# RWKV attention and a top-1 MoE on one core: u terms per block, other load order, states of 48 columns, row loads in two parts

## The chip, the cores and the metric

The kernel runs on one core of one Trainium2 chip. The metric is the device time of one execution in microseconds (us). A core has five engines that run their own instruction streams: TensorE (PE), VectorE (DVE), ScalarE (ACT), GpSimd (POOL) and SyncE (SP), which here issues nearly all DMA transfers. In a trace every fp32 matmul stands as two records. The profiler also gives the TensorE clock that was granted, as a share of full speed; in this trace it stands at 1.0 (2.4 GHz) or at 0.5 (1.2 GHz).

## The reference

The inputs have batch B = 4, H = 8 heads, S = 768 steps and head size D = 48. The attention part is a recurrence over steps, and its output, seen as 3072 tokens of 384 values, goes into a mixture of experts with one expert for each token:

```python
for t in range(S):
    cur = np.einsum('bhd,bhe->bhde', u[None] * kt, vt)
    y[:, :, t] = np.einsum('bhd,bhde->bhe', rt, state + cur)
    state = wt[:, :, :, None] * state + np.einsum('bhd,bhe->bhde', kt, vt)
x = attn_out.transpose(0, 2, 1, 3).reshape(B * S, H * D)
logits = x @ w_gate                      # 3072 x 8
expert_idx = np.argmax(logits, axis=1)
gate_w = softmax(logits)[arange, expert_idx]
for e in range(E):                       # 8 experts, 384 -> 1024 -> 384
    mask = expert_idx == e
    out[mask] = gate_w[mask, None] * (np.maximum(x[mask] @ w1[e], 0.0) @ w2[e])
```

## The kernel before, in words

**Attention.** The 768 steps are cut into 6 chunks of 128, so there are 24 blocks; block n has chunk c = n // 4 and batch b = n % 4. The 8 heads of a batch lie as 4 pairs; a pair takes 112 partitions, one head in 0 to 47, the other in 64 to 111. For each block the host packs w, r and k of all heads into one row tile `rkwt` (112 x 1544) and the values into `vt` (128 x 384). Per block:

- DVE forms products of decays by a scan (`suf`, L294), their reciprocal, `kh` (L301) and a second scan `pre` (L303). POOL forms `rk` (L286), the product of r and k that the u term needs, and `rh` (L315).
- PE multiplies `rh` and `kh` (L384, tile `ap`: the decayed products of all pairs of steps). POOL fills two tiles `at` with the u terms on the diagonal and zeros elsewhere (L365, from `ct`), and DVE copies the strict triangle of `ap` over them (L386). The u terms come from `rk` by a matmul with `ubt` (L340, `cp`), a copy on ACT (L343, `cs`), a transpose (L352, `cpt`) and a second copy on ACT (L354, `ct`).
- PE adds up the output `yp`: first the part from the state of the chunks before (`inter`, L395: the state `gbd` of a pair is a block-diagonal 112 x 112 matrix whose off-diagonal blocks are zero, one matmul for a pair), then the part within the chunk (`av`, L424: `at` by `vt`). ACT copies it to `ytb` (L428; in the first chunk L432).
- PE forms the chunk's contribution to the state (`ds`, L406, tile `dp`), DVE adds it into `sst` (L413, or copies it in chunk 0, L415), and ACT multiplies by the chunk's decay into `gbd` for the next chunk (`prep_g`, L331, 4 instructions for a block).
- `y_tr` (L440) transposes `ytb` into rows of tokens, ACT copies those to `xr`; once per chunk the logits (L456), the routing and the place of each token follow, and POOL scatters the rows by indirect DMA into `xs` in DRAM, one area for each expert (`scatter`). Before that, `prefill` has filled the rows that no token may reach (8 DMAs from `zrow`, L279).

**Experts.** The weights come in 20 pieces for an expert through 3 staging buffers `wst` (L182, L185), and ACT and DVE split them into a high and a low part (L195, L196). `load_rows` (L211) loads the rows of an expert, `xg`, from `xs`; the partition dimension of the load is 112, 116, 108, 103, 99 or 97 by the expert's capacity (128 for the last, and 96 and 128 for the two parts of the first). PE transposes them (L246), multiplies by w1 (L255) and w2 (L778), and an indirect DMA writes the result (L217). The transpose at L246 is the first thing that an expert does on PE.

**Order.** A tile scheduler orders PE, DVE, ACT and POOL by the dependences and the program's order. SP issues in program order: a DMA whose buffer isn't free yet holds everything that stands behind it on SP. In the loop over the blocks, `load(n + 5)` and `load_v(n + 5)` follow block n; a tag has 6 buffers.

Of the kernel before, what the change touches and what calls it, by code (L numbers as in the profile page):

```python
# [43 lines left out]
def rwkv_moe_kernel(ctx, tc, rkw, vv, ub, wgp, wg, w1, w2, out):  # L44
# [62 lines left out]
    make_identity(nc, ident)  # L107
    pre0 = []
# [14 lines left out]
    for b in range(B):  # L123
        gbd[b] = acon.tile([RP, NP_, RP], F32, name=f"gbd{b}")
        t = acon.tile([RP, NP_, RP], F32, name=f"sst{b}")
        nc.gpsimd.memset(t, 0.0)
        sst.append(t)
# [82 lines left out]
    def load_rows(t, e, row, n, p):  # L210
        i = nc.sync.dma_start(t, xs[e, row:row + n, :].rearrange("e (p j) c -> p (e j) c", p=p))  # L211
        for k in scat:
            tc.add_manual_dep(i.ins, k.name, mybir.DependencyInfo(mybir.DependencyClass.Sync, mybir.DependencyReason.DATA),
                              reason="rows of all tokens")
# [118 lines left out]
    def coef_mm(c, bs=range(B)):  # L333
        if c >= NCH:
            return
        nb = len(bs)
        cp = psL.tile([32 * nb, C], F32, name="cp", tag="lg")
# [4 lines left out]
        cs = sm.tile([32 * nb, C], F32, name="cs", tag="cs")  # L342
        nc.scalar.activation(cs, cp, AF.Copy)  # L343
        for b in bs:
            ch["cs", c, b] = cs

    def coef_tr(c, bs=range(B)):
        if c >= NCH:
            return
        nb = len(bs)  # L350
        cp = psL.tile([P, 32 * nb], F32, name="cpt", tag="lg")
        nc.tensor.transpose(cp, ch["cs", c, bs[0]], ident[:32 * nb, :32 * nb])  # L352
        ct = sm.tile([P, nb, 32], F32, name="ct", tag="ct")
        nc.scalar.activation(ct.rearrange("p b h -> p (b h)"), cp, AF.Copy)  # L354
        for i, b in enumerate(bs):
            ch["ct", c, b] = ct[:, i, :]

    def diag(n):
# [4 lines left out]
        co = ch["ct", n // B, n % B]  # L363
# [24 lines left out]
    def inter(n):  # L388
# [215 lines left out]
    def coefs(c, bs):  # L604
        coef_mm(c, bs)
        coef_tr(c, bs)

    C0 = {0: (1,), 1: (2, 3)}
    coefs(0, (0,))
    diag(0)  # L610
    prep_r(1)
    prep_rk(2)
    prep_rk(3)
    for n in range(NB):
        c, b = divmod(n, B)
        kt(n)
        if b == 0 and c > 0:
            diag(n)
# [3 lines left out]
        if n in C0:  # L622
            with hp():
# [383 lines left out]
```

## Time and profile before

| | us |
|---|---|
| three runs, lowest, median, highest | 521.66, 525.41, 527.87 |
| the profiled execution | 524.86 |
| its span from the first to the last instruction | 523.1 |
| PE busy in it (share) | 449.3 (86%) |
| DVE busy (share) | 308.5 (59%) |
| ACT and POOL busy (share) | 189.6 (36%) and 190.2 (36%) |
| mean granted clock of TensorE | 0.878 |

The lines of 40 slices on the page show the course: attention takes slices 1 to about 18 (13.1 us each), with DVE nearly full in many of them and PE's clock moving between 0.5 and 1; then come the experts, where PE is nearly full and the clock falls in single slices. A window's row gives the busy time of each engine in it, the number of records, the mean granted clock and the share of the 16 DMA engines. A timeline row gives the start, the time and the instruction, and in square brackets how long the engine had been idle before it and what it waited for.

### The profile page before, as it was taken

To read this page: it belongs to the slowest core of one execution; us is meant where nothing else is said; L and a number is where in the kernel's file an instruction comes from. 1 tells how busy PE (TensorE), PEld (TensorE's weight loads), DVE (VectorE), ACT (ScalarE), POOL (GpSimd) and SP (SyncE) were. 2 spreads that over 40 slices of the span, in tenths; PEclk is the share of its full clock that TensorE was granted. 3 is DMA by queue.
4 is the path that set the end of the run, shared out by engine and by line. 5 is a ranking of instruction groups with operands and counts; after the bars stand their busy time and mean duration, and the time that the engine had idled before them with its cause. 6 is when DMAs were issued, how large, how long until landed. Compare 5 with 4: busy or idle time off the path is not lost.

```text
span 523.1 us, 8844 instructions
## 1 busy us (share of the span) xinstructions
PE 449.3 (86%) x3323; PEld 399.2 (76%) x3323; DVE 308.5 (59%) x555; ACT 189.6 (36%) x447; POOL 190.2 (36%) x203
## 2 busy tenths in 40 slices
PE   6689979488798969799689999993999939999992
PEld 6466768367676758588689998883999929999992
DVE  6998467489979899654567525331646306261320
ACT  4262423343352353223535525332445205242210
POOL 7766252187485876350521002100303005230341
PEclk9585557787898989799979999996999978999998
DMA  8934434657443961410556244232643242410020
GB/s 228 282 126 138 143 119 141 187 204 201 137 139 102 297 168 58 171 47 18 166 205 223 82 164 134 58 112 98 181 152 115 80 136 82 142 41 5 3 51 36
DMA packets 35174, 67.68 MB, mean 129 GB/s; under 512 B 7636, under 2 KB 22909, under 8 KB 35124
## 3 DMA queue, kind: packets, MB, share of 16 engines
q1 hardware_dynamic: 27220, 57.52, 35.8%
q0 software_dynamic: 7904, 9.52, 5.7%
q8 instruction: 28, 0.46, 0.4%
q14 instruction: 22, 0.18, 0.1%
HBM read 51.81 MB, written 15.63 MB: 129 GB/s over the span
## 4 chain that ended last, share of the span: by engine, by line
issue 35%; PE 29%; DVE 17%; DMA 8%; POOL 5%; SPq 3%; ACT 1%; POOLq 0%; DVEq 0%; ACTq 0%
PE bank L255 6%; PE ap L384 5%; DMA rkwt<-in_rkw_dram 5%; POOL out_dram L217 4%; DVE suf L294 4%; PE yp L424 3%; PE opt L267 3%; DMA out_dram<-ot,xg 2%; DVE kh L301 2%; PE bank L778 2%; PE yp L395 2%; DVE pre L303 2%; DVE at L386 2%; PE yq L440 2%; PE lp L456 1%
## 5 line engine op out<-in xcount | busy, mean ns | idle before, releaser
L217 POOL DMA_INDIRECT out_dram<-ot,xg x24 | 37.2, 1551 | 177.0 <-DVE ot L768 171.5
L196 DVE TENSOR_TENSOR w2l<-wst,w2h 128x512 fp32r<-128x512 f32 x48 | 34.1, 745 | 64.4 <-ACT w2h L195 64.2
L384 PE MATMUL ap<-rh,kh 48*128 48x128 f32 (+1 forms) x384 | 61.8, 327 | 9.3 <-DVE pre L299 5.2
L384 PEld LDWEIGHTS ap<-rh,kh 48*128 48x128 f32 (+1 forms) x384 | 51.9, 224 | 19.1 <-DVE at L386 8.2
L255 PE MATMUL bank<-xl,w1h 128*128 128x448 f32 (+6 forms) x168 | 60.0, 361 | 0.0
L255 PE MATMUL bank<-xh,w1l 128*128 128x448 f32 (+6 forms) x168 | 58.6, 354 | 0.0
L255 PE MATMUL bank<-xh,w1h 128*128 128x448 f32 (+6 forms) x168 | 57.8, 368 | 0.3 <-ACT xh L247 0.3
L286 POOL TENSOR_TENSOR rk<-rkwt 112x512 f32<-112x512 f32 x24 | 37.0, 1542 | 31.3 <-DMA rkwt<-in_rkw_dram 20.2
L258 DVE SCALAR_TENSOR_TENSOR hl<-bank,hh 128x192 fp32r<-128x192 f32 (+8 forms) x58 | 30.5, 539 | 28.3 <-ACT hh L257 28.3
L424 PE MATMUL yp<-at,vt 128*48 128x128 f32 x384 | 40.7, 322 | 6.1 <-DVE at L386 6.1
L257 ACT ACTIVATE hh<-bank 128x192 fp32r<-128x192 f32 (+8 forms) x58 | 26.8, 477 | 42.7 <-PE bank L255 41.9
L365 POOL TENSOR_SCALAR_AFFINE_SELECT at<-ct 128x512 f32<-128x512 f32 x48 | 40.3, 866 | 5.0 <-PE yp L424 4.8
L294 DVE TENSOR_TENSOR_SCAN suf<-rkwt,sufone 112x520 f32<-112x520 f32 x24 | 38.8, 1619 | 5.4 <-DMA rkwt<-in_rkw_dram 5.2
L778 PE MATMUL bank<-hl,w2h 128*128 128x412 f32 (+5 forms) x114 | 40.8, 359 | 0.0
L778 PE MATMUL bank<-hh,w2l 128*128 128x412 f32 (+5 forms) x114 | 40.6, 358 | 0.0
L386 DVE COPY_PREDICATED at<-cmask,ap 128x512 f32<-128x512 int32 x48 | 34.2, 720 | 9.9 <-PE ap L384 9.1
L778 PE MATMUL bank<-hh,w2h 128*128 128x412 f32 (+5 forms) x114 | 39.8, 355 | 0.0
L196 DVE TENSOR_TENSOR w1l<-wst,w1h 128x512 fp32r<-128x512 f32 x48 | 31.0, 686 | 14.2 <-ACT w1h L195 14.1
L424 PEld LDWEIGHTS yp<-at,vt 128*48 128x48 f32 x384 | 28.0, 145 | 14.4 <-DVE at L386 8.8
L195 ACT ACTIVATE w2h<-wst 128x512 fp32r<-128x512 f32 x48 | 27.5, 623 | 31.6 <-DMA wst<-in_w_dram 28.9
L303 DVE TENSOR_TENSOR_SCAN pre<-rkwt,pre 112x520 f32<-112x520 f32 x24 | 35.1, 1461 | 4.7 <-POOL rh L315 4.1
L315 POOL TENSOR_TENSOR rh<-rkwt,pre 112x512 f32<-112x512 f32 x22 | 28.4, 1292 | 25.8 <-PE yp L395 16.9
(153 smaller groups left out, 928.2 us busy)
## 6 DMA issues: line engine op xcount, KB each, us to landing
rkwt<-in_rkw_dram SPq DMA_DIRECT2D x23, 675.5 KB, 18.7
wst<-in_w_dram SPq DMA_DIRECT2D x48, 256.0 KB, 5.6
wst<-in_w_dram SPq DMA_DIRECT2D x16, 768.0 KB, 7.5
xs<-zrow SPq DMA_DIRECT2D x7, 699.6 KB
vt<-in_vv_dram SPq DMA_DIRECT2D x24, 192.0 KB, 6.5
xg<-xs SPq DMA_DIRECT2D x1, 699.6 KB
xs<-zrow SPq DMA_DIRECT2D x1, 675.5 KB
xg<-xs SPq DMA_DIRECT2D x1, 675.5 KB
```

The source lines that it names most:

```text
L196: nc.vector.tensor_tensor(out=lo, in0=st[:, cs], in1=hi.bitcast(F32), op=ALU.subtract)
L217: i = nc.gpsimd.indirect_dma_start(out=out[:, :], out_offset=bass.IndirectOffsetOnAxis(ap=t.bitcast(I32)[:, q, DM + 1:DM + 2], axis=0), in ...
L255: nc.tensor.matmul(hp, a, x[:, j, :], start=(i == 0), stop=(i == 8))
L258: nc.vector.scalar_tensor_tensor(out=hl, in0=hp, scalar=0.0, in1=hh.bitcast(F32), op0=ALU.max, op1=ALU.subtract)
L286: return nc.gpsimd.tensor_tensor(out=d["rk"], in0=d["r"], in1=d["k"], op=ALU.mult)
L294: nc.vector.tensor_tensor_scan(out=suf[:, ::-1], data0=w[:, ::-1], data1=sufone.rearrange("p q c -> p (q c)")[:, ::-1], initial=0.0, op0=A ...
L303: nc.vector.tensor_tensor_scan(out=pre, data0=w, data1=p0.rearrange("p q c -> p (q c)"), initial=0.0, op0=ALU.mult, op1=ALU.add)
L365: nc.gpsimd.affine_select(out=at[:, j], in_=co[:, j:H:2].unsqueeze(2).broadcast_to([P, NP_, C]), pattern=[[0, NP_], [-1, C]], compare_op=A ...
L384: nc.tensor.matmul(ap[j][:, q, :], d["kh"][rs, q, :], d["rh"][rs, q, :], start=True, stop=True)
L386: nc.vector.copy_predicated(out=d["at"][:, j], mask=cmask.unsqueeze(1).broadcast_to([P, NP_, C]), data=ap[j])
L424: nc.tensor.matmul(yp[64 * j:64 * j + D, q, :], d["v"][:, h * D:(h + 1) * D], d["at"][:, j, q, :], start=(c == 0 and q == 0), stop=(q == N ...
L778: nc.tensor.matmul(pp, w, a, start=(i == 0), stop=(i == 23))
```

## The change

Four things are changed. (1) A row load whose partition count isn't a multiple of 16 becomes two: up to the last multiple of 16, and the rest. (2) `load` runs 6 blocks ahead instead of 5, `load_v` 3 instead of 5, `prefill` goes from blocks 0 to 7 to blocks 2 to 9, the first two scatters go to blocks 11 and 12. (3) The u terms are formed for each block, one block ahead: four matmuls put the four pairs into four column groups of one 128-row tile, ACT copies it whole, a matmul with the constant 128 x 8 matrix `pick` adds up what belongs to a head and transposes in one step, ACT copies the 128 x 8 result; `rk` is formed 2 blocks ahead instead of 4. (4) `gbd` and `sst` hold 48 columns for a head (and 64 in memory) in place of 112 with a zero half; `inter` becomes 8 matmuls of 64 or 48 rows instead of 4 of 112; `ds` fills 64 rows for the first head of a pair, and `sst` takes one DVE instruction over 112 partitions for a block in place of two over 48.

```diff
+    pick = const.tile([P, H], F32, name="pick")
+    nc.vector.tensor_reduce(out=pick, in_=ident.rearrange("p (q h) -> p h q", q=NP_)[:, 0:H, :], axis=AX.X, op=ALU.add)
...
-        gbd[b] = acon.tile([RP, NP_, RP], F32, name=f"gbd{b}")
-        t = acon.tile([RP, NP_, RP], F32, name=f"sst{b}")
-        nc.gpsimd.memset(t, 0.0)
-        sst.append(t)
+        gbd[b] = acon.tile([RP, NP_, 64], F32, name=f"gbd{b}")
+        sst.append(acon.tile([RP, NP_, D], F32, name=f"sst{b}"))
...
     def load_rows(t, e, row, n, p):
-        i = nc.sync.dma_start(t, xs[e, row:row + n, :].rearrange("e (p j) c -> p (e j) c", p=p))
+        src = xs[e, row:row + n, :].rearrange("e (p j) c -> p (e j) c", p=p)
+        m = p - p % 16
+        for ps in ((slice(0, m), slice(m, p)) if m < p else (slice(0, p),)):
+            i = nc.sync.dma_start(t[ps], src[ps])
...
-            nc.scalar.activation(d["g"][:, q, :], sst[n % B][:, q, :], AF.Copy, scale=d["wt"][:, q:q + 1])
+            nc.scalar.activation(d["g"][:, q, 0:D], sst[n % B][:, q, :], AF.Copy, scale=d["wt"][:, q:q + 1])
...
+    def coef_mm(n):
+        cp = psL.tile([P, C], F32, name="cp", tag="lg")
         for q in range(NP_):
-            for i, b in enumerate(bs):
-                nc.tensor.matmul(cp[32 * i:32 * i + 32, :], ubt[:, q, :], blk[c * B + b]["rk"][:, q, :],
-                                 start=(q == 0), stop=(q == NP_ - 1))
+            nc.tensor.matmul(cp[32 * q:32 * q + 32, :], ubt[:, q, :], blk[n]["rk"][:, q, :], start=True, stop=True)
+        cs = sm.tile([P, C], F32, name="cs", tag="cs")
         nc.scalar.activation(cs, cp, AF.Copy)
+        blk[n]["cs"] = cs
+
+    def coef_tr(n):
+        cp = psL.tile([P, H], F32, name="cpt", tag="lg")
+        nc.tensor.matmul(cp, blk[n]["cs"], pick, start=True, stop=True)
+        ct = sm.tile([P, H], F32, name="ct", tag="ct")
+        nc.scalar.activation(ct, cp, AF.Copy)
+        blk[n]["ct"] = ct
...
-                nc.tensor.matmul(yp[:, q, :], d["g"][:, q, :], d["rh"][:, q, :],
-                                 start=(q == 0), stop=False, skip_group_check=True)
+                for j in range(2):
+                    m = 64 if j == 0 else D
+                    rs = slice(64 * j, 64 * j + m)
+                    nc.tensor.matmul(yp[rs, q, :], d["g"][rs, q, 0:m], d["rh"][rs, q, :],
+                                     start=(q == 0), stop=False, skip_group_check=True)
...
-                    nc.tensor.matmul(dp[64 * j:64 * j + D, q, :], d["kt"][:, q * RP + 64 * j:q * RP + 64 * j + D],
+                    m = 64 if j == 0 else D
+                    nc.tensor.matmul(dp[64 * j:64 * j + m, q, :], d["kt"][:, q * RP + 64 * j:q * RP + 64 * j + m],
...
-            for j in range(2):
...
-                    nc.vector.tensor_tensor(out=s[rs, :, cs], in0=dp[rs], in1=d["g"][rs, :, cs], op=ALU.add)
...
+                nc.vector.tensor_tensor(out=s, in0=dp, in1=d["g"][:, :, 0:D], op=ALU.add)
...
+        with hp():
+            coefs(n + 1)
+        prep_rk(n + 2)
+        diag(n + 1)
...
-            if c > 1:
+            if c > 2:
                 scatter(c - 1)
...
-        load(n + 5)
-        load_v(n + 5)
-        if n == E:
-            scatter(0)
+        load(n + 6)
+        load_v(n + 3)
+        if n in (11, 12):
+            scatter(n - 11)
...
-        if n < E:
-            prefill(n)
+        if 2 <= n < 2 + E:
+            prefill(n - 2)
```

On SP, in the first blocks (rkwt are the packed inputs of a block, vt its values, xs the prefilled rows), the order before is this:

```order
L75 DMA rkwt<-in_rkw_dram 112x1544
L84 DMA vt<-in_vv_dram 128x384
L279 DMA xs<-zrow 448x1x386
L75 DMA rkwt<-in_rkw_dram 112x1544
L84 DMA vt<-in_vv_dram 128x384
L279 DMA xs<-zrow 464x1x386
```

and now:

```order
L75 DMA rkwt<-in_rkw_dram 112x1544 x4
L84 DMA vt<-in_vv_dram 128x384
L75 DMA rkwt<-in_rkw_dram 112x1544
...
L282 DMA xs<-zrow 448x1x386
L75 DMA rkwt<-in_rkw_dram 112x1544
L84 DMA vt<-in_vv_dram 128x384
```

Four packed inputs now go out in a row, the values stand three blocks behind them, and the prefill starts two blocks later.

On PE, one block of the second chunk (yq is the transpose of the block before, yp the block's output, dp the state's new part, kp a transpose of kh, ap the products of the next block) before:

```order
L340 MATMUL cp<-rk,ubt 32x128 x2
L440 MATMUL yq<-ident,ytb_203 128x112 x4
L395 MATMUL yp<-rh,gbd_189 112x128 x4
L406 MATMUL dp<-vt,kt 48x48 x8
L374 MATMUL kp<-ident,kh 128x112 x4
L424 MATMUL yp<-at,vt 48x128
L384 MATMUL ap<-rh,kh 128x128 x4
L424 MATMUL yp<-at,vt 48x128 x7
```

and the same place now:

```order
L340 MATMUL cp<-rk,ubt 32x128 x4
L368 MATMUL kp<-ident,kh 128x112 x4
L378 MATMUL ap<-rh,kh 128x128 x4
L435 MATMUL yq<-ident,ytb_201 128x112 x4
L392 MATMUL yp<-rh,gbd_189 64x128
L392 MATMUL yp<-rh,gbd_189 48x128
...
L347 MATMUL cpt<-pick,cs 128x8
L404 MATMUL dp<-vt,kt 64x48
L404 MATMUL dp<-vt,kt 48x48
```

The product with the state alternates between the two halves of the array (three more pairs of such rows are left out), the state's new part does the same, and the u terms' matmuls and their transpose by pick now stand in every block.

On SP in the experts (ISA rows are register work of the load), before:

```order
L702 TENSOR_LOAD order
L702 REGISTER_ALU x3
L702 ISA
L211 ISA
L211 DMA xg<-xs 103x1544
L185 ISA
L185 DMA wst<-in_w_dram 128x4x384
```

and now:

```order
L688 TENSOR_LOAD order
L688 REGISTER_ALU x3
L688 ISA
L214 ISA
L214 DMA xg<-xs 96x1544
L214 ISA
L214 DMA xg<-xs 7x1544
L185 ISA
L185 DMA wst<-in_w_dram 128x4x384
```

The one load of 103 partitions has become one of 96 and one of 7, at the same place ahead of the weights.

## Rows read from the trace of the kernel before

**Rows 1.** The head of the page: span, busy time of each engine, and the line of the granted clock over 40 slices.

```profile
span 523.1 us, 8844 instructions
...
PE 449.3 (86%) x3323; PEld 399.2 (76%) x3323; DVE 308.5 (59%) x555; ACT 189.6 (36%) x447; POOL 190.2 (36%) x203
...
PEclk9585557787898989799979999996999978999998
```

**Rows 2.** Busy time by stretch of the attention part: window, its length, busy us and records of PE, PEld, DVE, ACT and POOL, granted clock, DMA share, GB/s. Block 0 ends about the end of the first row; the rows then hold blocks 1 to 3, 4 to 7, 8 to 19 and 20 to 23.

```profile
0.00:30.30 30.30, 21.46 (x190) 17.39 (x191) 25.81 (x39) 10.03 (x25) 21.94 (x46) 0.72 0.82 226
30.30:55.20 24.90, 22.47 (x162) 16.70 (x162) 21.45 (x28) 11.37 (x31) 14.50 (x14) 0.70 0.46 143
55.20:106.40 51.20, 40.95 (x347) 32.73 (x348) 30.54 (x53) 19.38 (x53) 18.29 (x22) 0.68 0.51 157
106.40:210.50 104.10, 89.59 (x966) 73.87 (x966) 95.74 (x165) 43.38 (x123) 71.90 (x75) 0.89 0.53 161
210.50:238.00 27.50, 24.26 (x216) 19.39 (x216) 15.14 (x38) 5.78 (x17) 10.61 (x14) 0.88 0.30 104
```

**Rows 3.** Timeline of ACT: the copies of yp to ytb that end blocks 7 and 19.

```profile
106.35 0.60 ACT L428 ACTIVATE ytb<-yp 112x512 f32<-112x512 f32 x1 [0.72 <-PE yp L424]
...
210.49 0.58 ACT L428 ACTIVATE ytb<-yp 112x512 f32<-112x512 f32 x1
```

**Rows 4.** Timeline of PE in the experts: the first transposes of the rows of two experts.

```profile
361.12 0.58 PE L246 MATMUL pt<-ident,xg 103*128 103x103 f32 x2 [9.11 <-DMA xg<-xs]
...
431.79 0.56 PE L246 MATMUL pt<-ident,xg 97*128 97x97 f32 x2 [9.27 <-DMA xg<-xs]
```

**Rows 5.** Timeline of SP: when the loads of those rows were issued.

```profile
332.17 0.29 SPq L211 DMA_DIRECT2D xg<-xs  x1
...
404.53 0.29 SPq L211 DMA_DIRECT2D xg<-xs  x1
```

**Rows 6.** Windows in the experts, columns as in rows 2: one while the first of the two loads runs, and the stretches right behind the two waits.

```profile
336.00:338.00 2.00, 2.00 (x11) 1.80 (x10) 0.00 (x0) 0.00 (x0) 0.00 (x0) 1.00 0.07 28
...
361.00:364.30 3.30, 3.18 (x12) 3.07 (x13) 0.61 (x2) 1.27 (x3) 0.00 (x0) 0.50 0.07 27
...
431.80:436.00 4.20, 4.20 (x16) 4.20 (x17) 1.63 (x3) 2.29 (x5) 0.00 (x0) 0.50 0.08 28
```

**Rows 7.** SP's own waits over the whole span: waited for, total us, times, longest.

```profile
SPq L84 <- PE yp L424: 82.9, 12, 11.8
...
SPq L84 <- PE dp L406: 27.4, 4, 10.5
```

**Rows 8.** Timelines of SP, ACT, PE and POOL about the end of the second chunk.

```profile
86.90 6.62 SPq L182 DMA_DIRECT2D wst<-in_w_dram  x3
...
99.96 0.63 ACT L195 ACTIVATE w1h<-wst 128x512 fp32r<-128x512 f32 x1 [7.38 <-DMA wst<-in_w_dram]
...
101.13 1.01 PE L440 MATMUL yq<-ident,ytb 112*128 112x112 f32 x4 [6.96 <-ACT ytb L428]
...
103.40 1.85 POOL L286 TENSOR_TENSOR rk<-rkwt 112x512 f32<-112x512 f32 x1 [10.05 <-DMA rkwt<-in_rkw_dram]
```

**Rows 9.** Groups of instructions by line and form over the whole span: count, busy us, mean ns of one, idle time before them and what ended it.

```profile
L331 ACT ACTIVATE gbd<-sst,wtot 112x112 f32<-112x112 f32 x80 | 25.4, 378 | 28.8 <-DVE sst L413 28.1 <-PE yp L395 0.5
...
L413 DVE TENSOR_TENSOR sst<-dp,gbd 48x192 f32<-48x192 f32 x32 | 11.2, 349 | 1.9 <-PE dp L406 1.7
...
L415 DVE COPY sst<-dp 48x192 f32<-48x192 f32 x8 | 2.7, 343 | 0.1
...
L459 ACT ACTIVATE ls<-lp 128x128 f32<-128x128 f32 x6 | 1.6, 272 | 3.7 <-PE lp L456 3.7
...
L352 PE MATMUL cpt<-ident,cs 128*128 128x128 f32 x5 | 1.6, 329 | 0.0
```

**Rows 10.** Timeline of PE in the second chunk: the products with the state (L395), within the chunk (L384, L424), each line so many records in a row. The first two stand in stretches at clock 0.5, the other three in one at 1.0.

```profile
61.97 2.05 PE L395 MATMUL yp<-rh,gbd 112*112 112x128 f32 x8
...
82.89 1.80 PE L395 MATMUL yp<-rh,gbd 112*112 112x128 f32 x8
...
85.63 1.71 PE L384 MATMUL ap<-rh,kh 48*128 48x128 f32 x16
...
88.58 1.04 PE L395 MATMUL yp<-rh,gbd 112*112 112x128 f32 x8
89.55 1.08 PE L424 MATMUL yp<-at,vt 128*48 128x128 f32 x16
```

**Rows 11.** Windows between changes of the clock, from block 2 to block 6, columns as in rows 2.

```profile
40.20:61.90 21.70, 20.72 (x145) 15.05 (x144) 15.14 (x22) 7.38 (x20) 8.80 (x8) 0.50 0.48 152
61.90:64.00 2.10, 2.10 (x11) 2.03 (x11) 0.00 (x0) 1.40 (x4) 0.00 (x0) 0.51 0.27 97
64.00:67.30 3.30, 1.81 (x30) 1.22 (x28) 2.86 (x9) 2.05 (x7) 3.13 (x5) 1.00 0.47 121
67.40:82.80 15.40, 13.99 (x88) 10.99 (x89) 9.85 (x22) 2.38 (x5) 5.05 (x6) 0.50 0.37 121
...
84.50:94.20 9.70, 9.38 (x114) 7.59 (x112) 7.04 (x8) 3.90 (x11) 4.96 (x6) 1.00 0.47 143
```

**Rows 12.** Timeline of DVE in the first blocks: the two masked copies that finish the first block's at.

```profile
22.55 0.74 DVE L386 COPY_PREDICATED at<-cmask,ap 128x512 f32<-128x512 int32 x1
...
25.59 0.73 DVE L386 COPY_PREDICATED at<-cmask,ap 128x512 f32<-128x512 int32 x1
```

More of the change, by code (lines that the diff above doesn't have):

```diff
@@ L210, in load_rows @@
     def load_rows(t, e, row, n, p):
-        i = nc.sync.dma_start(t, xs[e, row:row + n, :].rearrange("e (p j) c -> p (e j) c", p=p))
-        for k in scat:
-            tc.add_manual_dep(i.ins, k.name, mybir.DependencyInfo(mybir.DependencyClass.Sync, mybir.DependencyReason.DATA),
-                              reason="rows of all tokens")
+        src = xs[e, row:row + n, :].rearrange("e (p j) c -> p (e j) c", p=p)
+        m = p - p % 16
+        for ps in ((slice(0, m), slice(m, p)) if m < p else (slice(0, p),)):
+            i = nc.sync.dma_start(t[ps], src[ps])
+            for k in scat:
+                tc.add_manual_dep(i.ins, k.name, mybir.DependencyInfo(mybir.DependencyClass.Sync, mybir.DependencyReason.DATA),
+                                  reason="rows of all tokens")
     def scatter_out(t, q, rows):
@@ L330, in prep_g @@
         for q in range(NP_):
-            nc.scalar.activation(d["g"][:, q, :], sst[n % B][:, q, :], AF.Copy, scale=d["wt"][:, q:q + 1])
[L333 to L337, printed above, removed]
+            nc.scalar.activation(d["g"][:, q, 0:D], sst[n % B][:, q, :], AF.Copy, scale=d["wt"][:, q:q + 1])
+    def coef_mm(n):
+        cp = psL.tile([P, C], F32, name="cp", tag="lg")
         for q in range(NP_):
-            for i, b in enumerate(bs):
-                nc.tensor.matmul(cp[32 * i:32 * i + 32, :], ubt[:, q, :], blk[c * B + b]["rk"][:, q, :],
-                                 start=(q == 0), stop=(q == NP_ - 1))
-        cs = sm.tile([32 * nb, C], F32, name="cs", tag="cs")
+            nc.tensor.matmul(cp[32 * q:32 * q + 32, :], ubt[:, q, :], blk[n]["rk"][:, q, :], start=True, stop=True)
+        cs = sm.tile([P, C], F32, name="cs", tag="cs")
         nc.scalar.activation(cs, cp, AF.Copy)
[L344 to L356, printed above, removed]
+        blk[n]["cs"] = cs
[5 more added lines that the diff above has]
+        blk[n]["ct"] = ct
     def diag(n):
@@ L362, in diag @@
         at = wk.tile([P, 2, NP_, C], F32, name="at", tag="at")
-        co = ch["ct", n // B, n % B]
+        co = blk[n]["ct"]
         for j in range(2):
@@ L572, in rwkv_moe_kernel @@
     prep_r(0)
-    for n in range(3, 5):
+    for n in range(3, 6):
         load(n)
-        load_v(n)
     prep_c(1)
@@ L602, in hp, with coefs @@
         return tc.high_priority(offset=60)
[L604 to L609, printed above, removed]
+    def coefs(n):
+        if n >= NB:
+            return
+        coef_mm(n)
+        coef_tr(n)
+    coefs(0)
     diag(0)
     prep_r(1)
-    prep_rk(2)
-    prep_rk(3)
     for n in range(NB):
@@ L616, in rwkv_moe_kernel @@
         kt(n)
-        if b == 0 and c > 0:
-            diag(n)
         if b == 1 and c > 0:
@@ L621, in rwkv_moe_kernel @@
         prep_w(n + 2)
-        if n in C0:
-            with hp():
-                coefs(0, C0[n])
-        prep_rk(n + 4)
-        if b < 3:
-            diag(n + 1)
+        with hp():
+            coefs(n + 1)
+        prep_rk(n + 2)
+        diag(n + 1)
         prep_r(n + 2)
@@ L644, in rwkv_moe_kernel @@
         av(n)
-        load(n + 5)
-        load_v(n + 5)
-        if n == E:
-            scatter(0)
-        if b == 3:
-            with hp():
-                coefs(c + 1, range(B))
+        load(n + 6)
+        load_v(n + 3)
+        if n in (11, 12):
+            scatter(n - 11)
         if n == 0:
```

8 lines of the change are left out of this document (3 added, 5 removed).

## The prediction, made before the change was run

> **What bounds the kernel now.** I read the head of the page first: PE is busy for 449.3 of 523.1 us, DVE for 308.5, and the granted clock goes up and down over the whole span [rows 1]. PE is what the time is made of, but a PE at half clock is as busy as one at full clock, so the share alone tells little; the windows by stretch tell more [rows 2]. Blocks 8 to 19 take 104.10 us, 8.67 a block, with DVE busy for 95.74 of them: this stretch is bound by DVE. The ends of blocks 7 and 19 on ACT give the same length, 104.14 us [rows 3]. Blocks 4 to 7 take 51.20 us, 12.8 a block, with no engine near full (PE 40.95, DVE 30.54) at clock 0.68: this stretch waits. Blocks 0 to 3 take 55.2 us at clocks of 0.72 and 0.70, and the last four blocks 27.5 us with PE at 24.26.
>
> In the experts I looked for idle time of PE. Two waits stand out: 9.11 and 9.27 us for the rows of an expert, of 103 and 97 partitions [rows 4]. Their loads had been issued 29 and 27 us before (361.12 less 332.17, 431.79 less 404.53) [rows 4, 5]. While the first runs, the DMA share is 0.07 at 28 GB/s, one sixteenth of the engines [rows 6]. The Trainium skill says the same of the count of engines (DMA: Bandwidth & Descriptors, "How many engines (k)": the largest k up to 16 that divides the slowest dimension), so that 103 and 97 would get one and 96 sixteen; the 0.07 agrees.
>
> **The change, part by part.** The sum is made against the profiled execution, 524.86 us, which is 0.55 below the median of the runs shown (525.41).
>
> *Row loads.* A load of 96 partitions and a small rest replaces one of 103 or 97. Both waits go, if the larger part comes in less than the 20 us that PE doesn't notice (29 less 9.11): 9.11 + 9.27 = 18.4 us. Behind each wait PE works at clock 0.50 for 3.30 and 4.20 us, fully busy [rows 6]; at full clock that is half, so 1.6 + 2.1 = 3.7 us more. **-22**, ends -18 (waits alone) and -24 (weights behind the slow load also come earlier). What is late next on these experts is the split of the weights on ACT and DVE; nothing in the rows shows it within 10 us, so I give it nothing.
>
> *Order on SP.* SP waits 82.9 + 27.4 us for the values' buffers (`load_v` waits for PE's last reader of the buffer) [rows 7], and behind it stand the packed inputs and the weights. The place where that reaches the other engines is the end of the second chunk: a group of three weight loads is held on SP for 6.62 us at 86.90; ACT, in order, then waits 7.38 us for a weight piece, so the copy of `yp` behind it is late and PE waits 6.96 us for it; POOL waits 10.05 us for packed inputs [rows 8]. Now inputs go out one block earlier and values only where their buffer has long been free. Blocks 4 to 7 without the 7 us would take 44.2; at the pace of blocks 8 to 19 they would take 4 x 8.67 = 34.7, a gain of 16.5; if the clock stays at half they take (see rival B) at least 4 x 11.5 = 46, a gain of 5. I take the middle, **-11**, ends -5 and -16.5. The prefill moves with it, from blocks 0 to 7 to blocks 2 to 9, away from the first loads.
>
> *Start.* The two masked copies that finish the first block's `at` stand at 22.55 and 25.59, with a scan and copies of other blocks between them [rows 12], because DVE is nearly full there (25.81 of 30.30 us [rows 2]). In the new order both stand directly one after the other, and the u terms of one block alone come earlier: **-3**, ends 0 and -6 (3.0 us between the copies, and as much for the rest).
>
> *DVE.* `sst` takes one instruction for two. Sixteen additions of 349 ns and four copies of 343 ns go: 7.0 us in all [rows 9], if one of 112 partitions takes as long as one of 48 (free size 192 in both). On the path they count where DVE bounds, in blocks 8 to 19: 12 x 0.35 = **-4.2**, ends 0 and -7. The one reduction for `pick` lies in the wait for the first inputs: 0.
>
> *PE.* The product with the state has 16 records a block instead of 8. No row shows that shape. Eight records of 112 x 112 took 1.04 us at full clock; sixteen of `av` 1.08, sixteen of `ap` (also 48 rows, both halves in turn) 1.71 [rows 10]. So a block pays between 0.04 and 0.67, or 1.04 if each of the new records takes as long as one of the old (16 x 0.13 = 2.08). The u terms add about 18 transposes by `pick`, 36 records of at most 329 ns (the old transpose [rows 9]), 12 us in all at the worst, some 0.5 a block. Both lie beside DVE's work in blocks 8 to 19, where PE is busy for 89.59 of 104.10 and DVE sets the pace; they count where PE does. I take the price of `ap`, its nearest relative in rows, on five blocks: **+3**, ends 0 and +20 (all blocks at 1.04). The Trainium skill has a rule against this step (TensorEngine Tiling (Array Packing), Gotcha 1: PSUM Pressure): two row tiles can't use the same PSUM bank at once, and here both halves write the bank of one `yp`, while the halves of `ap` go to two. By it the price would be nearer 1.04 a block, and the term about +5 in place of +3.
>
> *ACT and POOL.* ACT gets a copy of 128 x 128 (272 ns for its like [rows 9]) and a small one per block, and `prep_g` writes 48 columns where it wrote 112 (378 ns each, four a block [rows 9]); it is busy for 43.38 of 104.10, so 0. POOL loses four fills at the start: 0.
>
> *A new wait.* The buffers of the token rows (`xr`) are two. The copies of the third chunk's rows now need the first scatter, which stands on POOL behind block 11's `rh` and after all prefill. **+1**, ends 0 and +4.
>
> *Clock.* Not only idle time lowers it. PE was busy for 20.72 of 21.70 us at clock 0.50, and for 13.99 of 15.40 [rows 11]; each rise in these rows comes behind the eight records of 112 x 112 (61.97 and 82.89 [rows 10], then 1.00 from 64.00 and 84.50 [rows 11]). The new records use a smaller part of the array. **+2** for falls that last longer; the other end is rival B. The Trainium skill (TensorE: Matmul & The Clock Gate, Part 1) ties the clock to how busy PE has recently been; by that a fuller PE would only gain, and the 21.70 us row speaks against it.
>
> Sum: -22 - 11 - 3 - 4.2 + 3 + 1 + 2 = -34.2; 524.9 - 34.2 = 490.7, with the median 0.55 higher **491 us**.
>
> **The rivals.**
>
> *A: the attention part doesn't move.* What DVE and SP give is taken up by PE's additions and by DMAs that collide (inputs earlier against prefill later). For it: the last four blocks and blocks 1 to 3 have PE near full, where more records cost. Against it: the wait at 94 to 101 us has a plain cause on SP. Only the row loads stay: 525.4 - 22 = 503.
>
> *B: slower, the clock.* Without the full-array product the clock stays at half through chunks 1 to 5. Work per block: 89.59 / 12 = 7.47 us busy at 0.89, or 6.65 at full clock; the same eight records take 1.80 to 2.05 at half against 1.04, a factor of 1.73 to 1.97, so a block takes 11.5 to 13.1, say 12.3. Sixteen such blocks are 197, the last four (24.26 x 0.88 x 1.85) about 40: 237 against 51.2 + 104.1 + 27.5 = 182.8, so +54; with -22 and -3 it is **554**. Each block at half costs 12.3 - 8.67 = 3.6, so it eats the whole gain from about 10 of 20 blocks on, and the kernel is slower by over 1% from 11. For it: rows 11. Against it: blocks 0 to 3 have no such product (none in chunk 0) and run at 0.72 and 0.70 [rows 2], not 0.5.
>
> *C: attention at the pace of its best stretch.* Blocks 4 to 7 gain 16.5, the start 6, DVE 7, the additions lie beside other work: 525.4 - 24 - 16.5 - 6 - 7 = 472.
>
> *D: the split brings nothing.* The two parts run one after the other on the same engines. The Trainium skill advises against splitting a transfer into disjoint partition halves (DMA: Bandwidth & Descriptors, Rules for kernel authors), as both would spray over all engines; here the unsplit load has one engine by its 0.07, so the advice doesn't reach it. It would leave 525.4 - 13 = 512.
>
> **How the numbers follow.** A measurement of this kernel can tell about 1% (5 us) from no change: the runs shown lie within 1.2%. Chances: the forecast (480 to 497) 0.53; A (498 to 509) 0.20; C (below 480) 0.13; D 0.03; B 0.11, of which 0.04 end within 1% because only part of the blocks run at half. Predicted 491. The range leaves out B, most of D and the far end of C: **471 to 509**. Faster by over 1% (below 520): 0.53 + 0.20 + 0.13 + 0.03 = 0.89, less 0.01 for what I haven't seen: 0.88; within 1%: 0.05; slower: 0.07.
>
> **What would show it.** Row loads: no idle time of over 2 us before L246's first records, DMA share well over 0.07 behind the issue. SP: waits at the values' load near nothing, blocks 4 to 7 under 45 us. DVE: 24 instructions of `sst` of about 350 ns. PE: 16 records with the state, 1.1 to 2.1 us at full clock. Clock: windows of chunks 1 to 5 at 0.85 or more; if they show 0.5 to 0.7 with PE busy, B holds. I would be wrong if the stretch of blocks 8 to 19 got longer than 104 us, or if the waits at the row loads turned into waits for weights of the same length.

## The result, and the profile after

The changed kernel takes 506.38 us (median of 4 runs, 503.82 to 513.33) against 526.61 us before (4 runs): a ratio of 0.961, 95% interval 0.954 to 0.968. It is 20 us faster; forecast were 34. The profiled execution of the changed kernel is its slowest (513.33 us, mean clock 0.846 where the others had 0.849 to 0.858), and a ratio in this document leaves out, on both sides, every execution over 1.5% above its kernel's fastest, which a median of times doesn't. So the stretches below show what happens, and the timed experiments say how much it is worth.

The head of the page of the changed kernel, for [rows 1]:

```profile
span 511.6 us, 9304 instructions
...
PE 468.6 (92%) x3523; PEld 405.3 (79%) x3523; DVE 283.0 (55%) x536; ACT 189.9 (37%) x479; POOL 192.6 (38%) x199
...
PEclk9555595775596559959997999999999999999997
```

PE is busy for 19 us more in a span that is 11.5 us shorter, DVE for 25.5 us less. Of DVE's 25.5 us the additions to the state are 7; most of the rest stands in instructions that the change leaves as they were (the scan `suf` takes 1308 ns instead of 1619 in the mean, `kh` 828 instead of 980), and no run here shows why. The low digits of the clock behind the two waits of [rows 4] (6 in slice 28, 7 and 8 in slices 33 and 34) are gone from the experts, and low digits stand thicker in the attention part. The same by stretch, for [rows 2] (columns as there; the rows are block 0, blocks 1 to 3, and then four blocks each):

```profile
0.00:26.40 26.40, 17.55 (x166) 14.56 (x167) 21.47 (x36) 10.15 (x24) 18.25 (x39) 0.74 0.94 242
26.40:59.05 32.65, 32.65 (x206) 25.59 (x206) 23.81 (x31) 14.42 (x45) 25.61 (x22) 0.50 0.60 175
59.05:97.39 38.34, 35.22 (x367) 26.87 (x366) 28.07 (x53) 15.93 (x51) 21.42 (x23) 0.76 0.52 163
97.39:147.07 49.68, 41.19 (x343) 30.83 (x344) 23.25 (x46) 17.52 (x53) 22.39 (x25) 0.66 0.60 178
147.07:189.27 42.20, 41.85 (x364) 31.07 (x364) 30.41 (x59) 16.48 (x54) 24.98 (x25) 0.61 0.51 158
189.27:220.78 31.51, 27.60 (x364) 21.30 (x364) 24.74 (x48) 10.46 (x38) 19.24 (x21) 0.93 0.28 90
220.78:246.64 25.86, 25.86 (x274) 19.33 (x275) 10.91 (x32) 5.02 (x15) 8.81 (x11) 0.86 0.14 51
```

The same bounds of blocks for blocks 8 to 15 in the kernel before, which [rows 2] hold in one row with four more:

```profile
106.35:145.34 38.99, 31.71 (x287) 26.53 (x287) 36.15 (x59) 14.54 (x41) 25.90 (x29) 0.79 0.55 167
145.34:178.21 32.87, 30.15 (x336) 24.28 (x336) 28.43 (x51) 14.61 (x42) 23.42 (x23) 0.94 0.54 161
```

Block 0 ends 4 us earlier, blocks 4 to 7 shrink from 51.2 to 38.3 us, and then blocks 8 to 15 take 91.9 us where they took 71.9. The attention part as a whole ends at 246.6 instead of 238.0; all of the gain is in the experts, 265.0 us (511.6 less 246.64) instead of 285.1.

There the two waits of [rows 4] are gone. Groups of the row transposes for those experts, idle time behind the second bar:

```profile
L249 PE MATMUL pt<-ident,xg 103*128 103x103 f32 x12 | 1.6, 251 | 0.0
L249 PE MATMUL pt<-ident,xg 97*128 97x97 f32 x12 | 1.5, 249 | 0.0
```

And this is what stands ahead of block 8 and in it now. Timelines of SP, ACT and POOL of the changed kernel:

```profile
75.65 0.70 SPq L282 DMA_DIRECT2D xs<-zrow  x1
76.51 9.13 SPq L75 DMA_DIRECT2D rkwt<-in_rkw_dram  x1
...
86.20 0.71 SPq L282 DMA_DIRECT2D xs<-zrow  x1
87.08 9.07 SPq L75 DMA_DIRECT2D rkwt<-in_rkw_dram  x1
...
96.91 0.70 SPq L282 DMA_DIRECT2D xs<-zrow  x1
97.67 10.04 SPq L182 DMA_DIRECT2D wst<-in_w_dram  x3
...
106.16 0.72 ACT L325 ACTIVATE junk<-rkwt,wmin 112x512 bf16<-112x512 f32 x1 [7.77 <-DMA rkwt<-in_rkw_dram]
...
115.66 0.63 ACT L195 ACTIVATE w1h<-wst 128x512 fp32r<-128x512 f32 x1 [7.19 <-DMA wst<-in_w_dram]
...
115.60 1.19 POOL L552 DMA_INDIRECT xs<-xr,pi  x1 [12.06 <-DMA wst<-in_w_dram]
```

ACT waits 7.8 us for packed inputs and 7.2 us for weights, POOL 12.1 us at the first scatter. The two loads of inputs that take 9 us to issue, and the three of weights that take 10, each follow a prefill on SP. A prefill of 464 rows is a DMA from 116 partitions. While one runs alone, the DMA share is about a quarter:

```profile
104.00:106.00 2.00, 0.00 (x0) 0.00 (x0) 0.82 (x1) 0.00 (x0) 0.00 (x0) 1.00 0.26 89
```

A share of 0.26 is about 4 engines of 16; at 89 GB/s its 699.6 KB take 8 us, an estimate. The Trainium skill's rule on the count of engines (DMA: Bandwidth & Descriptors, "How many engines (k)") gives 4 for 116 partitions, which the 0.26 agrees with. It is the same handicap that the change takes off the row loads, left on the prefill.

### The profile page after: what moved, and what is told of

It reads as the page before. It is cut to its first block, busy times and chain, and to the rows that moved or that the text cites. A ratio compares the mean times of both kernels' runs of the same rounds, so it can differ in the third digit from the quotient of the medians.

```text
span 511.6 us, 9304 instructions
## 1 busy us (share of the span) xinstructions
PE 468.6 (92%) x3523; PEld 405.3 (79%) x3523; DVE 283.0 (55%) x536; ACT 189.9 (37%) x479; POOL 192.6 (38%) x199
## 4 chain that ended last, share of the span: by engine, by line
PE 41%; issue 33%; DMA 9%; POOL 7%; DVE 6%; ACT 1%; SPq 1%; POOLq 0%; ACTq 0%; DVEq 0%
PE ap L378 8%; PE yp L419 6%; PE bank L258 5%; PE yp L392 4%; POOL out_dram L220 4%; DMA wst<-in_w_dram 4%; DMA out_dram<-ot,xg 3%; PE yq L435 3%; PE bank L764 2%; PE opt L270 2%; PE dp L404 2%; PE kp L368 2%; PE cp L340 2%; POOL xs L552 2%; DMA rkwt<-in_rkw_dram 2%
## 5 line engine op out<-in xcount | busy, mean ns | idle before, releaser
L378 PE MATMUL ap<-rh,kh 64*128 64x128 f32 (+1 forms) x384 | 61.2, 367 | 0.1
L378 PEld LDWEIGHTS ap<-rh,kh 64*128 64x128 f32 (+1 forms) x384 | 48.5, 250 | 13.2 <-issue 10.7
L258 PE MATMUL bank<-xh,w1h 128*128 128x448 f32 (+6 forms) x168 | 56.2, 358 | 1.2 <-ACT xh L250 1.2
L359 POOL TENSOR_SCALAR_AFFINE_SELECT at<-ct 128x512 f32<-128x512 f32 x48 | 43.2, 921 | 27.4 <-PE yp L419 16.4
L196 DVE TENSOR_TENSOR w2l<-wst,w2h 128x512 fp32r<-128x512 f32 x48 | 32.0, 702 | 36.5 <-ACT w2h L195 36.3
L419 PE MATMUL yp<-at,vt 128*48 128x128 f32 x384 | 46.9, 346 | 2.6 <-DVE at L380 2.5
L260 ACT ACTIVATE hh<-bank 128x192 fp32r<-128x192 f32 (+8 forms) x58 | 26.8, 477 | 43.7 <-PE bank L258 42.8
L419 PEld LDWEIGHTS yp<-at,vt 128*48 128x48 f32 x384 | 31.1, 155 | 9.2 <-issue 3.9
L306 DVE TENSOR_TENSOR_SCAN pre<-rkwt,pre 112x520 f32<-112x520 f32 x24 | 33.0, 1377 | 8.8 <-POOL rh L318 8.5
L552 POOL DMA_INDIRECT xs<-xr,pi x24 | 26.1, 1086 | 31.3 <-DVE ks L520 12.9
L195 ACT ACTIVATE w1h<-wst 128x512 fp32r<-128x512 f32 x48 | 28.6, 629 | 23.7 <-DMA wst<-in_w_dram 11.5
## 6 DMA issues: line engine op xcount, KB each, us to landing
xs<-zrow SPq DMA_DIRECT2D x7, 699.6 KB
```

The source lines that it names most:

```text
L196: nc.vector.tensor_tensor(out=lo, in0=st[:, cs], in1=hi.bitcast(F32), op=ALU.subtract)
L258: nc.tensor.matmul(hp, a, x[:, j, :], start=(i == 0), stop=(i == 8))
L306: nc.vector.tensor_tensor_scan(out=pre, data0=w, data1=p0.rearrange("p q c -> p (q c)"), initial=0.0, op0=ALU.mult, op1=ALU.add)
L359: nc.gpsimd.affine_select(out=at[:, j], in_=co[:, j:H:2].unsqueeze(2).broadcast_to([P, NP_, C]), pattern=[[0, NP_], [-1, C]], compare_op=A ...
L378: nc.tensor.matmul(ap[j][:, q, :], d["kh"][rs, q, :], d["rh"][rs, q, :], start=True, stop=True)
L419: nc.tensor.matmul(yp[64 * j:64 * j + D, q, :], d["v"][:, h * D:(h + 1) * D], d["at"][:, j, q, :], start=(c == 0 and q == 0), stop=(q == N ...
```

## The experiments

The theories at first: **1**, the product with the state in quarters of the array keeps the clock at half; **2**, the waits in block 8 lower it; **3**, the u terms per block load PE and ACT.

**Single parts.** Part four of the change undone, and each of parts four, two and three alone in the kernel before (diffs as in the change):

```diff
-                for j in range(2):
-                    nc.tensor.matmul(yp[rs, q, :], d["g"][rs, q, 0:m], d["rh"][rs, q, :], ...)
+                nc.tensor.matmul(yp[:, q, :], d["g"][:, q, :], d["rh"][:, q, :], ...)
```

> The changed kernel with its fourth part undone: block-diagonal states of 112 columns, one full-array product with the state for a pair, two DVE instructions for sst. Theory 1 (the product in quarters of the array keeps the clock at half): blocks 8 to 15, 91.9 us in the changed kernel with 67 us of them at clock 0.5, come back to 72 to 78 us with less than 30 us at 0.5, although DVE has 7 us more work; the time falls from 506 to 487 to 495 us. Theory 2 (the wait in block 8 for late inputs, prefill and the first scatter lowers the clock, and nothing about the product matters): blocks 8 to 15 stay at 88 us or more, time 505 to 512 us. Theory 3 (the u terms per block load PE and ACT): as theory 2.

> The kernel before with the fourth part alone (states of 48 columns, product in quarters). Theory 1: the clock of blocks 8 to 19 falls from 0.89 to 0.75 or less, that stretch grows from 104 to 115 to 125 us, time 535 to 550 us against 526.6. Theories 2 and 3: DVE's 4.2 us come off, time 520 to 527 us, clock as before.

> The kernel before with the second part alone (inputs 6 blocks ahead, values 3, prefill in blocks 2 to 9, first scatters at blocks 11 and 12). Theory 1: blocks 4 to 7 shrink by 8 to 12 us and the rest stays, time 514 to 519 us. Theory 2: that gain is given back by the waits in block 8 and a longer stretch at clock 0.5 behind them, blocks 8 to 15 grow from 72 to 85 us or more, time 525 to 535 us. Theory 3 says the same as theory 1.

> The kernel before with the third part alone (u terms for each block, rk two blocks ahead). Theory 3: PE waits for cs on ACT in many blocks and 36 more records, blocks 8 to 15 grow by 8 us or more, time 533 to 545 us. Theories 1 and 2: a little at the start either way, 522 to 529 us.

Undoing part four gave 497.1 us (4 runs, no ratio), 9 us faster than the complete change. Two of its runs, 492.4 and 494.2, lie in theory 1's range, the other two, 500.0 and 504.9, in neither; blocks 8 to 15 took 85.2 us with 34 at clock 0.5, in neither theory's range. The states alone gave 519.9, ratio 0.988 (0.983 to 0.993): theory 1 falls in the form in which it stood there, since blocks 8 to 19 took 108.9 us at a clock of 0.83, not 115 to 125 at 0.75. The order alone gave 515.2, 0.976 (0.971 to 0.981), as theories 1 and 3 said of the time. But not all the rest stayed: blocks 4 to 7 fell to 32.5 us, and blocks 8 to 15 grew to 82.4 and blocks 1 to 3 to 31.2. The u terms alone gave 527.3, 0.997 (0.991 to 1.003): nothing, so theory 3 falls.

So the parts alone are worth -11, -6 and +1 by the medians (-13, -6 and -2 by the ratios), the first two as forecast or better, and together, beside the row loads, nearly nothing. The next four runs looked for the pair that spoils it.

> The kernel before with the first part alone (row loads split at a multiple of 16 partitions). All theories: the two waits of 9.1 and 9.3 us go and the clock doesn't fall behind them, the experts take about 265 us instead of 285, time 503 to 508 us against 526. Were the split not to spread over the engines: 520 or more.

> The changed kernel with its third part undone (u terms per chunk, rk four blocks ahead), so rows, order and states. The parts alone gave -6 (states), -11 (order), +1 (u terms), and rows should give -20. Theory 4 (states in quarters and u terms per block together leave PE with too little work on the whole array, so the clock stays down): without the u terms per block the loss goes, time 487 to 495 us, blocks 8 to 15 at 80 us or less. Theory 5 (states in quarters lose with the new order, by the wait in block 8 behind which the clock can't come back): the loss stays, 501 to 508 us, blocks 8 to 15 at 86 us or more.

> The changed kernel with its second part undone (inputs and values 5 blocks ahead, prefill in blocks 0 to 7, scatter after block 8), so rows, u terms and states. Theory 4: the loss of states with u terms stays, time 511 to 519 us, more than 55 us at clock 0.5 in blocks 8 to 15. Theory 5: the loss goes with the order, 498 to 504 us, and blocks 8 to 15 have less than 40 us at clock 0.5.

The row loads alone gave 503.75, ratio 0.958 (0.951 to 0.964), 21.3 us: all theories' number, and as much as the whole change. This run changes no line of the attention part, and still its windows differ from those of the kernel before; blocks 4 to 7, 8 to 11 and 12 to 15:

```profile
59.52:107.45 47.93, 36.79 (x344) 29.39 (x342) 32.50 (x53) 18.00 (x51) 17.80 (x21) 0.75 0.48 148
107.45:146.35 38.90, 33.48 (x287) 27.85 (x287) 34.60 (x58) 14.50 (x40) 27.46 (x29) 0.75 0.54 168
146.35:184.28 37.93, 35.86 (x357) 28.25 (x357) 28.64 (x53) 14.50 (x41) 22.80 (x24) 0.81 0.49 148
```

So a window of one execution can move by some 5 us, and its clock by 0.13, without a cause in the code there, and differences of that size between windows show little.

Without the u terms the complete change took 499.55, 0.951 (0.944 to 0.958); without the order 499.81, 0.950 (0.943 to 0.957). Theory 4's time was missed in the one (its blocks 8 to 15, 71.8 us, were met), theory 5's time was met in the other (its time at clock 0.5 was just missed, 42.8 us where it said under 40), and the two runs together speak against either: whichever of the three parts is left out, 7 to 9 us come back by the medians. By the ratios it is 5 to 6 us for these two runs, with intervals that overlap a little with that of the complete change. No pair is shown to be to blame.

**Work for the clock.** Four matmuls of zeros per block from chunk 1 on, on 112 x 112 of the array, and as a control on a corner of 64 x 64:

```diff
+            for q in range(NP_):
+                nc.tensor.matmul(yp[:, q, :], zst, d["rh"][:, q, :], start=False, stop=False, skip_group_check=True)
```

> The changed kernel with four matmuls more in each block from chunk 1 on: a 112 x 112 matrix of zeros times rh, added to the same output, which changes no value. It is work on the whole array that nothing needs, 8 records a block, 1.04 us at full clock, 21 us in all. If the clock is what was lost, and work on the whole array brings it back: blocks 8 to 15 fall from 91.9 to 72 to 82 us, with less than 40 us at clock 0.5 against 67, and the time is 493 to 502 us in spite of the additional work. If waits make the loss and the clock only follows them: the work adds up where PE bounds, 508 to 525 us.

> The control to the run with matmuls of zeros on the whole array: the same number of additional matmuls (four in each block from chunk 1 on), but of a 64 x 64 corner of zeros. It changes no value. If work on the whole array is what raised the clock there (0.895 against 0.846 to 0.858 in the changed kernel): the clock stays at 0.87 or less, more than 45 us at 0.5 in blocks 8 to 15, time 508 to 520 us. If any work on PE does it: clock 0.89 or more, less than 35 us at 0.5 in blocks 8 to 15, 500 to 507 us.

The run with the whole array gave 505.9 us at a mean clock of 0.895, the control 508.1 at 0.893. The first met what was said of the clock (30 us at 0.5 in blocks 8 to 15, which took 82.3 us) and missed the time of both theories; the control met the time of the one theory, with 46 us at 0.5 in these blocks, and the mean clock of the other. Windows of blocks 8 to 11 and 12 to 15, first with zeros on the whole array, then in the corner:

```profile
104.14:150.19 46.05, 41.58 (x398) 32.32 (x398) 28.41 (x51) 17.65 (x54) 29.51 (x28) 0.74 0.54 166
150.19:186.48 36.29, 32.41 (x379) 25.47 (x381) 27.59 (x53) 15.25 (x50) 23.27 (x25) 0.91 0.59 177
```

```profile
96.60:148.23 51.63, 36.53 (x373) 28.22 (x374) 36.06 (x55) 17.73 (x56) 25.76 (x29) 0.78 0.53 163
148.23:188.55 40.32, 38.78 (x393) 30.79 (x392) 26.55 (x53) 15.79 (x50) 22.05 (x23) 0.71 0.52 157
```

Either kind of additional work raised the mean clock from about 0.855, so the shape isn't shown to be the cause; in blocks 12 to 15 the whole array stands higher (0.91 against 0.71), in one execution each. And neither bought time: at a clock of 0.74 and 0.78, against 0.66 in the changed kernel, blocks 8 to 11 still take 46 and 52 us, with PE busy for 90% and 71% of them. Something else holds that stretch.

**The prefill.** Theory 6: the prefill on 4 engines delays the inputs behind it. The prefill is split as the change splits the row loads, in the changed kernel and in the one with part four undone:

```diff
+        m = rows - rows % 16
+        for lo, hi in ((0, m), (m, rows)) if m < rows else ((0, rows),):
+            nc.sync.dma_start(xs[e, 4 * lo:4 * hi, :]..., zrow[lo:hi]...)
```

> The changed kernel with the prefill of 464 rows (116 partitions) split into 112 and 4 partitions, as the change does with the row loads. Theory 6 (each prefill of 116 partitions moves on 4 engines at about 91 GB/s for 8 us, and the next load of inputs stands 9 us in issue behind it, so the inputs of blocks 9 to 12 come late and the gain of the other parts is given back there): loads of inputs are issued in under 1 us, waits for inputs and weights between 92 and 120 us go, blocks 4 to 11 shrink from 88.0 to 70 to 80 us, time 490 to 500 against 506. Theory 1 (only the clock counts, the waits don't): time 502 to 509, blocks 8 to 15 with more than 55 us at clock 0.5.

> The changed kernel with full-array states (part four undone) and the prefill split. Theory 6: 8 to 14 us faster than part four undone alone (497), 482 to 490 us. Theory 1: at 497 or little below, 493 to 499. Against the changed kernel with the prefill split alone this one tells whether the product in quarters still costs when inputs come in time: by theory 1 it is 8 us or more faster, by theory 6 within 4 us of it.

The changed kernel with it takes 488.84 us, ratio 0.931 (0.926 to 0.935), 17.5 us less. SP's timeline of that run at the same place as above:

```profile
71.65 1.38 SPq L284 DMA_DIRECT2D xs<-zrow  x2
80.20 0.35 SPq L75 DMA_DIRECT2D rkwt<-in_rkw_dram  x1
...
82.77 1.39 SPq L284 DMA_DIRECT2D xs<-zrow  x2
84.22 2.65 SPq L182 DMA_DIRECT2D wst<-in_w_dram  x3
87.19 0.33 SPq L75 DMA_DIRECT2D rkwt<-in_rkw_dram  x1
```

Loads behind a prefill are issued in 0.35 us instead of 9. Between the first prefill and the load behind it SP now waits until the load's buffer is free (73.03 to 80.20 us): it is ahead of the blocks and no longer behind them. Its windows, by the same blocks as after the change:

```profile
0.00:26.30 26.30, 16.84 (x166) 13.66 (x167) 21.48 (x36) 10.04 (x24) 18.57 (x39) 0.70 0.94 233
26.30:58.96 32.66, 32.66 (x209) 25.59 (x209) 23.80 (x31) 14.43 (x46) 25.60 (x22) 0.51 0.82 234
58.96:89.52 30.56, 28.80 (x351) 22.31 (x349) 25.91 (x50) 15.75 (x51) 21.21 (x22) 0.89 0.82 228
89.52:122.75 33.23, 30.46 (x386) 22.93 (x382) 26.11 (x49) 16.86 (x52) 29.02 (x28) 1.00 0.63 192
122.75:164.62 41.87, 37.09 (x340) 27.96 (x340) 31.61 (x59) 16.81 (x55) 22.52 (x24) 0.67 0.53 161
164.62:196.94 32.32, 29.92 (x375) 22.89 (x376) 23.68 (x48) 10.62 (x38) 19.07 (x23) 0.90 0.21 69
196.94:219.33 22.39, 21.94 (x264) 16.51 (x263) 10.71 (x32) 5.00 (x16) 8.12 (x10) 1.00 0.24 85
```

Blocks 4 to 11 take 63.8 us where they took 88.0, and of all waits for inputs and weights there one of 4.7 us is left, on ACT; time and length are a little better than theory 6 said, and theory 1 falls. With part four undone it is 488.79, 0.929 (0.923 to 0.935): the same. With inputs in time the shape of the product costs nothing, as theory 6 said and theory 1 didn't. That isn't because nothing depends on it: in blocks 12 to 15 the run with full states has DVE busy for 41.87 of 42.72 us,

```profile
124.59:167.31 42.72, 34.05 (x358) 26.84 (x356) 41.87 (x67) 17.04 (x55) 28.42 (x31) 0.88 0.63 182
```

and the one with states of 48 columns takes 41.87 us with DVE at 31.61 and the clock at 0.67: two limits of nearly the same length.

The last run asks whether the three other parts are worth something now:

> The kernel before with the row loads split (503.8 alone) and the prefill split, without the parts on order, u terms and states. Theory 6 (the prefill ate what those three parts give: with it split, they are worth 10 us or more): 498 to 504 us, 10 to 15 above the changed kernel with the prefill split (488.8). Theory 7 (the prefill's 15 us are there in any order, and the three parts are worth nothing with or without it): 486 to 491 us.

It took 491.7 us, 0.932 (0.921 to 0.942), next to theory 7 and far from theory 6's 498 to 504. So the prefill's gain is there in either order, 12 us without the three parts and 17.5 with them, and the three parts together are worth 3 us with it and minus 3 without it, neither clear of the intervals. The prefill is not what ate the three parts. Its windows of blocks 1 to 3, 4 to 7, 8 to 11 and 12 to 15:

```profile
30.30:54.58 24.28, 24.28 (x166) 18.66 (x165) 20.05 (x29) 11.42 (x32) 13.35 (x13) 0.63 0.66 184
54.58:93.44 38.86, 32.33 (x358) 25.88 (x357) 31.93 (x55) 17.71 (x51) 16.54 (x20) 0.87 0.68 187
93.44:133.58 40.14, 33.84 (x271) 27.77 (x272) 33.68 (x56) 14.61 (x42) 26.09 (x30) 0.70 0.55 159
133.58:166.97 33.39, 30.76 (x356) 24.82 (x356) 29.27 (x52) 14.60 (x41) 24.16 (x24) 0.95 0.54 163
```

Against these the change with the prefill split gains 4.0 us in block 0 (26.30 against 30.30), 8.3 in blocks 4 to 7 and 6.9 in blocks 8 to 11, where the parts were meant to help. It loses 8.4 us in blocks 1 to 3 and 8.5 in blocks 12 to 15, where the clock is 0.51 against 0.63 and 0.67 against 0.95. One execution of each stands behind this, but over all the profiles the same is seen. Blocks 1 to 3 take 30.3 to 32.7 us in the ten with the new order or the u terms per block, 24.3 to 28.7 in the four without either. Blocks 12 to 15 take 36.3 to 42.7 us in the eight with the new order and 29.4 to 38.0 in the six without.

The fastest version, at 488.8 us, is the change with the prefill split, with either form of the states.

## Why the prediction was right, and where it was not

It held in its sign, its range (471 to 509) and its largest term. Its sum, 491, was missed by 15 us: 506 lies outside the forecast's own interval (480 to 497) and in that of rival A (498 to 509), which the range took in. A sign that it named for being wrong came true: blocks 8 to 19 got longer than 104 us, 123.4 in the changed kernel (sum of three windows), 107.4 with the prefill split. By its own steps:

- **Row loads, -22: right.** Alone they measure -21.3; the waits are gone, and the experts take 20 us less. The half-clock stretches behind the waits had to be in the sum: the waits alone were 18.4.
- **Order on SP, -11: right alone, wrong in its reason and in company.** Alone it gave -10.9, and in the changed kernel blocks 4 to 7 lost 12.9 us against [rows 2]. But the step "the place where that reaches the other engines is the end of the second chunk" took SP's 6.62 us at 86.90 [rows 8] for a result of the values' buffers. It stands right behind a prefill, as do the loads of inputs that took 9 us to issue. Timeline of SP of the kernel before, which the prediction read for the wait alone:

```profile
46.67 8.60 SPq L75 DMA_DIRECT2D rkwt<-in_rkw_dram  x1
...
55.83 0.70 SPq L279 DMA_DIRECT2D xs<-zrow  x1
56.63 9.12 SPq L75 DMA_DIRECT2D rkwt<-in_rkw_dram  x1
...
86.14 0.71 SPq L279 DMA_DIRECT2D xs<-zrow  x1
```

  With the prefill split and the order as before (the last run) blocks 4 to 7 take 38.86 us, where the row loads alone left 47.93: so the prefill had about 9 us of that stretch. Moving the prefill "away from the first loads" was counted as a help. It moved seven slow DMAs two blocks later, the last from 96.23 to 96.91 us while the blocks had come forward, onto the loads of blocks 8 and on and in front of the first scatter. In the changed kernel the gain of blocks 4 to 7 was given back in blocks 8 to 11, which took 10.7 us more than before and 16.5 more than with the prefill split.
- **A new wait, +1 with an end of +4: the place right, the path and the size not.** POOL itself waited 12.06 us at the first scatter, and 0.17 with the prefill split. No copy of rows waits for a scatter in the trace, which is what the step had priced.
- **DVE, -4.2: the price right, the place and the cover wrong.** The 16 additions over 112 partitions take 346 ns each, as those over 48 did [rows 9]:

```profile
L408 DVE TENSOR_TENSOR sst<-dp,gbd 112x192 f32<-112x192 f32 x16 | 5.5, 346 | 5.9 <-PE dp L404 5.9
```

  The states alone gave -6, but not where the step had put it. Blocks 8 to 19 took 108.89 us there against 104.10 [rows 2]:

```profile
97.89:206.78 108.89, 96.66 (x1088) 74.46 (x1086) 91.27 (x157) 43.49 (x131) 75.33 (x80) 0.83 0.52 159
```

  The gain stands in blocks 0, 4 to 7 and 20 to 23 (about 3, 5 and 7 us), so the near number is luck. And DVE's relief counts only while DVE sets the pace. In the changed kernel it is busy for 162.7 us of the attention part instead of 188.7, PE for 221.9 instead of 198.7 (sums of the windows): in blocks 12 to 15 PE is busy for 41.85 of 42.20.
- **PE, +3 for more records: too high.** Sixteen records in quarters took 1.08 us at full clock, the lower bound, and a transpose by `pick` 0.39:

```profile
193.24 1.08 PE L392 MATMUL yp<-rh,gbd 64*64 64x128 f32 x16
...
195.25 0.29 PE L347 MATMUL cpt<-pick,cs 128*128 128x8 f32 x2
...
200.78 0.39 PE L347 MATMUL cpt<-pick,cs 128*128 128x8 f32 x2
```

  The Trainium skill's rule on row tiles and a common PSUM bank (TensorEngine Tiling (Array Packing), Gotcha 1: PSUM Pressure), by which it would have been near 2.08, doesn't show in the 1.08. PE's work as such didn't grow: busy time times granted clock, summed over the windows, an estimate, is 160 us before [rows 2], 157 after and 158 with the prefill split.
- **Clock, +2: the term that was mis-sized most.** As PE's work is the same by that estimate, the 23 us of additional busy time in attention are the clock's. In blocks 12 to 15 alone, where PE has nearly no idle time left, the stretch grew from 32.9 to 42.2 us as the clock fell from 0.94 to 0.61. With the prefill split it is still 41.87 us at 0.67, against 33.39 at 0.95 without the three parts. Rival B's mechanism is not shown as it was told: neither the states alone nor the two runs with the prefill split, with either form of the states, make the product in quarters its cause.
- **Start, -3: given back.** Block 0 ends 3.9 us earlier. Blocks 1 to 3 then run with PE busy without a gap at clock 0.50 and take 32.65 us instead of 24.90 [rows 2]. The u terms alone do the same: block 0 ends at 25.0 us, and blocks 1 to 3 take 31.3.

So the time fell into the range because of its first term. What happened to the rest was rival A, which had a chance of 0.20: everything but the row loads adds up to +3 by the medians (506.4 against 503.75), not clear of the intervals. A's reason, "DMAs that collide", is half of the story. They do collide: splitting the prefill gives 17.5 us in the changed kernel and 12 without the three parts. But with the prefill split the three parts still give only 3. What takes up their 19 us in blocks 0 and 4 to 11 is blocks 1 to 3 and 12 to 15 at a lower clock, which stood in the sum with +2; A names blocks 1 to 3, but for more records and not for the clock.

Open: what holds or lifts the clock in a stretch where PE is busy all the time, why the new order and the u terms lower it in blocks 1 to 3, and why the complete change loses 5 to 9 us to any version that lacks one of its three parts. Undoing part four keeps the stalls on SP (9.15, 9.08 and 10.40 us at the same places) and is still 9 us faster, so the stalls alone don't explain it. The order in which clock and waits fall on the blocks differs from one run to the next by several us, and no run here separates them.

## What to carry to other kernels

When a DMA is slow for the count of its partitions, look for every other DMA with the same handicap before moving any of them: the one that isn't on the critical path holds the queue for those that are. Parts that each gain alone needn't add up when they relieve different engines of one loop: compare stretch by stretch what each gives and what it costs, and ask which engine is full in each, and at what clock. A long issue on SP is to be read together with the DMA just ahead of it on the queue, not only with the semaphore that it might wait for.

## What the runs showed that was not expected

PE was busy for 32.65 of 32.65 us at clock 0.50 in blocks 1 to 3 of the changed kernel, and for 32.66 at 0.51 in the run with the prefill split. The Trainium skill (TensorE: Matmul & The Clock Gate, Part 1: The HAM clock gate) ties the clock to how busy PE has recently been; the busy share of the trace doesn't decide it here. More work of either shape raised the mean clock by some 0.04 and bought no time. And a DMA of 116 partitions held the issue of a load behind it on SP for up to 9.13 us; with 112 and 4 partitions in its place the same load was issued in 0.35.
